# Moving the stream's buffers from 32 bytes below a 4 KB boundary of the partition onto one

## The chip, the cores and the metric

One core of one Trainium2 chip runs the kernel; the other cores are idle. The metric is the device time of the kernel in microseconds (us). Runs of the kernels before and after differ by about 0.05% among themselves, so a difference of 1% is far above the noise; of the experiments, e4 and e12 spread over 0.2% and e11 over 0.9%.

## The reference, cut to what matters

A decode step: layernorm and modulation, grouped-query attention over a long cache, then a small MLP. What costs is reading memory once: 134 MB of K and V cache and 44 MB of weights.

```python
x: (2, 1, 1024)
k_cache, v_cache: (2, 4, 32768, 128) bf16        # 67 MB each
w_mod (1024, 6144), wq (1024, 4096), wo (4096, 1024), w1 (1024, 3584), w2 (3584, 1024)
scores = einsum('bhqd,bhkd->bhqk', q, k) * Dh ** -0.5
p = softmax(scores); o = einsum('bhqk,bhkd->bhqd', p, v)
```

## The kernel before

All big loads form one stream, issued in a fixed order by SyncE (SP) into a ring of 160 KB a partition. Most loads are 2 MB: 128 partitions, 16 KB each in one contiguous run. A load waits only until the tiles that overlap its place in the ring have been read.

```python
RING = 160 * 1024
...
ident = sb("ident", [128, 128], BF16)          # the first of some 60 small tensors
# ... [cut] ...
KT_sb = [sb(f"KT_sb{i}", [128, 8, 128], BF16) for i in range(NKT)]

arena = nc.alloc_sbuf_tensor("arena", [128, RING], mybir.dt.uint8)   # comes last
abase = nc.lookup_mloc(arena).addr             # 61,408 = 15 * 4096 - 32
# ... [cut] ...
SLOT = {("K", 0): 0, ("K", 1): 1, ("V", 0): 2, ("V", 1): 3, ("K", 2): 4, ("V", 2): 5, ("K", 3): 6, ("V", 3): 7}

def add_kv(kind, i, cc):                       # 8192 keys, 64 to a partition: 16 KB in one run
    cache = A_k_cache if kind == "K" else A_v_cache
    b, g = i % 2, i // 2
    r0 = cc * CH_ROWS
    add((kind, i, cc), [TPC, D], cache[b, g][r0:r0 + CH_ROWS, :].rearrange("(p t) d -> p t d", p=128),
        SLOT[kind, cc] * 16 * KB, f"{kind}{cc}")
# ... [cut] ...
def need(*key):                                # issues the stream up to the item asked for
    ...
        T.dma("sp", lambda e, dst=dst, src=cur.src: e.dma_start(dst, src), key=cur.sem, writes=[cur.reg], frees=old)
```

The offsets of all items in the ring are multiples of 1 KB, and so are their rows (7 KB, 8 KB, 12 KB or 16 KB). So the place of `abase` modulo 1 KB is the place of every packet of the stream.

## Time and profile before

| | before |
|---|---|
| time, median of 3 runs | 430.73 us (430.69 to 430.78) |
| load queue q1, share of 16 engines' span | 98.4% |
| bytes moved, mean rate | 178.6 MB, 416 GB/s |
| PE / DVE / ACT busy | 68% / 38% / 36% |

From the page of the kernel before: DMA busy share and rate in 40 equal slices of the span, the packets, the load queue (q1), the chain of waits by engine, and the issues of the K loads (KB each, median us from issue to landing).

```profile
DMA  8999999999999999999999999999999999999993
GB/s 330 428 418 418 428 419 429 422 424 425 428 428 428 428 428 425 428 428 428 427 428 428 428 425 429 426 429 425 429 426 427 428 428 427 428 424 412 419 416 155
DMA packets 14471, 178.61 MB, mean 416 GB/s; under 512 B 1768, under 2 KB 1775, under 8 KB 2799
...
q1 hardware_dynamic: 14112, 178.27, 98.4%
...
DMA 79%; PE 17%; ACT 1%; SPq 1%; DVE 1%; issue 1%; DVEq 0%; ACTq 0%
...
K<-in_A_k_cache_dram SPq DMA_DIRECT2D x32, 2048.0 KB, 32.2
```

Every slice but the first and the last has the DMA engines busy. A 2 MB load takes about 4.9 us of them but lands 32 us after its issue, so several loads always queue. The table of stages (busy us and instruction count of PE, PEld, DVE, ACT, POOL, then granted clock, DMA share, GB/s) says the same for the steady stretch of the kernel before: all engines have slack, DMA has none.

```profile
120.00:350.00 230.00, 178.81 (x3441) 155.04 (x3434) 112.69 (x214) 108.63 (x191) 1.14 (x6) 0.90 1.01 427
```

### The profile page before, as it was taken

How to read it: one execution, taken by the hardware profiler on the slowest of the kernel's cores; microseconds unless marked ns; L12 is line 12 of the kernel's file. 1: busy time of each engine (PE TensorE's matmuls, PEld its weight loads, DVE VectorE, ACT ScalarE, POOL GpSimd, SP SyncE). 2: the span in 40 equal slices, each digit the busy share in tenths (PEclk: the TensorE clock that was granted, in tenths of full speed). 3: DMA queues.
4: the chain of work that ended last, by engine and by line, in shares of the span. 5: the costliest groups of instructions: out<-in, count | busy, mean ns of one | idle time of the engine just before them, and what ended most of it. 6: DMA issues, size and time to landing. Idle time of an engine off the chain costs nothing.

```text
span 429.0 us, 13364 instructions
## 1 busy us (share of the span) xinstructions
PE 289.7 (68%) x6035; PEld 253.2 (59%) x6035; DVE 162.9 (38%) x340; ACT 155.0 (36%) x266; POOL 2.8 (1%) x17
## 2 busy tenths in 40 slices
PE   0643368968997689678777858895878671644644
PEld 0632368956875688477576837784866661243543
DVE  0200026534574366247436524761564343102100
ACT  1100016438556338244634543481437335100100
POOL 1000000000000000000000000000000000000000
PEclk9999999868999979889969898897989886655555
DMA  8999999999999999999999999999999999999993
GB/s 330 428 418 418 428 419 429 422 424 425 428 428 428 428 428 425 428 428 428 427 428 428 428 425 429 426 429 425 429 426 427 428 428 427 428 424 412 419 416 155
DMA packets 14471, 178.61 MB, mean 416 GB/s; under 512 B 1768, under 2 KB 1775, under 8 KB 2799
## 3 DMA queue, kind: packets, MB, share of 16 engines
q1 hardware_dynamic: 14112, 178.27, 98.4%
q8 instruction: 16, 0.26, 0.2%
q10 hardware_dynamic: 334, 0.02, 0.1%
q14 instruction: 9, 0.07, 0.0%
HBM read 178.28 MB, written 0.00 MB: 416 GB/s over the span
## 4 chain that ended last, share of the span: by engine, by line
DMA 79%; PE 17%; ACT 1%; SPq 1%; DVE 1%; issue 1%; DVEq 0%; ACTq 0%
DMA K<-in_A_k_cache_dram 59%; PE psKT L476 11%; DMA wo<-in_A_wo_dram 8%; DMA w<-in_B_w_dram 7%; DMA wmod<-in_w_mod_dram 5%; PE psS L488 3%; PE psO L518 1%; SPq L373 1%; ACT KT_sb L480 1%; PE psS L612 0%; ACT E_sb L509 0%; PE psO L646 0%; ACT L509 0%; DVE KT_sb L482 0%; PE psM L422 0%
## 5 line engine op out<-in xcount | busy, mean ns | idle before, releaser
L476 PE MATMUL psKT<-ident,K 128*128 128x128 bf16 x2048 | 175.2, 238 | 42.5 <-DMA K<-in_A_k_cache_dram 42.5
L476 PEld LDWEIGHTS psKT<-ident,K 128*128 128x128 bf16 x2048 | 134.3, 106 | 52.8 <-DMA K<-in_A_k_cache_dram 49.3
L480 ACT ACTIVATE KT_sb<-psKT 128x1024 bf16<-128x1024 bf16 x96 | 97.9, 1020 | 175.3 <-PE psKT L476 175.1
L482 DVE COPY KT_sb<-psKT 128x1024 bf16<-128x1024 bf16 x160 | 108.5, 690 | 121.7 <-PE psKT L476 120.6
L488 PE MATMUL psS<-qcur,KT_sb 128*128 128x8 bf16 x2048 | 88.8, 168 | 9.8 <-ACT KT_sb L480 7.1
L488 PEld LDWEIGHTS psS<-qcur,KT_sb 128*128 128x128 bf16 x2048 | 80.1, 99 | 15.5 <-ACT KT_sb L480 9.4
L518 PE MATMUL psO<-V,E_sb 128*32 128x512 bf16 x512 | 36.5, 412 | 3.8 <-DMA V<-in_A_v_cache_dram 3.0
L509 ACT ACTIVATE E_sb<-S_sb,negm 128x256 bf16<-128x256 f32 x64 | 32.3, 504 | 9.8 <-DVE negm L505 8.9
L493 DVE TENSOR_REDUCE m1c<-S_sb 128x8 f32<-128x512 f32 x32 | 21.9, 686 | 14.7 <-ACT S_sb L492 13.6
L492 ACT ACTIVATE S_sb<-psS 128x512 f32<-128x512 f32 x32 | 19.0, 592 | 13.3 <-PE psS L488 13.3
L518 PEld LDWEIGHTS psO<-V,E_sb 128*32 128x32 bf16 x512 | 11.6, 101 | 15.1 <-DMA V<-in_A_v_cache_dram 4.1
L447 PE MATMUL psS<-siluT,wmod 128*128 128x2 bf16 x384 | 11.2, 165 | 8.5 <-DMA wmod<-in_w_mod_dram 7.0
L455 PE MATMUL psO<-hT,wq 128*128 128x2 bf16 x256 | 7.5, 165 | 12.9 <-DMA wq<-in_A_wq_dram 12.9
L447 PEld LDWEIGHTS psS<-siluT,wmod 128*128 128x128 bf16 x384 | 10.9, 104 | 8.9 <-DMA wmod<-in_w_mod_dram 7.3
L612 PE MATMUL psS<-atT,wo 128*128 128x2 bf16 x256 | 7.5, 165 | 12.4 <-DMA wo<-in_A_wo_dram 12.4
L612 PEld LDWEIGHTS psS<-atT,wo 128*128 128x128 bf16 x256 | 7.1, 104 | 13.3 <-DMA wo<-in_A_wo_dram 13.3
L455 PEld LDWEIGHTS psO<-hT,wq 128*128 128x128 bf16 x256 | 7.1, 104 | 13.2 <-DMA wq<-in_A_wq_dram 13.2
L424 ACT ACTIVATE stat<-stat 128x2 f32<-128x2 f32 x3 | 0.6, 203 | 37.1 <-DVE stat L423 37.1
L646 PE MATMUL psO<-gT,w 128*128 128x2 bf16 x224 | 6.6, 165 | 9.8 <-DMA w<-in_B_w_dram 9.8
L646 PEld LDWEIGHTS psO<-gT,w 128*128 128x128 bf16 x224 | 6.3, 104 | 10.1 <-DMA w<-in_B_w_dram 10.1
L509 ACT ACTIVATION_READ_ACCUMULATOR E_sb<-S_sb,negm 128x1 f32 x64 | 12.1, 189 | 0.0
L628 PE MATMUL psS<-h2T,w 128*128 128x2 bf16 x224 | 7.8, 172 | 3.4 <-DMA w<-in_B_w_dram 2.2
(85 smaller groups left out, 86.1 us busy)
## 6 DMA issues: line engine op xcount, KB each, us to landing
K<-in_A_k_cache_dram SPq DMA_DIRECT2D x32, 2048.0 KB, 32.2
V<-in_A_v_cache_dram SPq DMA_DIRECT2D x32, 2048.0 KB, 35.7
wmod<-in_w_mod_dram SPq DMA_DIRECT2D x8, 1536.0 KB, 17.5
wq<-in_A_wq_dram SPq DMA_DIRECT2D x4, 2048.0 KB, 38.2
wo<-in_A_wo_dram SPq DMA_DIRECT2D x4, 2048.0 KB, 27.6
w<-in_B_w_dram SPq DMA_DIRECT2D x4, 1792.0 KB, 38.3
w<-in_B_w_dram SPq DMA_DIRECT2D x3, 2048.0 KB, 31.5
w<-in_B_w_dram SPq DMA_DIRECT2D x1, 1024.0 KB, 29.8
```

Source lines behind the costliest of these rows:

```text
L447: pe(lambda e, w=it.view, j=j, k=k: e.matmul(psS[0][:, 2 * j:2 * j + 2], lhsT=w[:, j * 128:(j + 1) * 128], rhs=siluT[:, :, k], start=(k == ...
L455: pe(lambda e, w=it.view, h=h, k=k: e.matmul(psO[:, 2 * h:2 * h + 2], lhsT=w[:, k % 2, h * 128:(h + 1) * 128], rhs=hT[:, k, :], start=(k = ...
L476: pe(lambda e, kq=kq, jj=jj, w=it.view, t=t: e.transpose(psKT[kq][:, jj * 128:(jj + 1) * 128], w[:, t, :], ident[:, :]), reads=[it.reg, "i ...
L480: act(lambda e, src=src: e.activation(KT_sb[g8][:, :, :], src, ACT.Copy), reads=[f"psKT{kq}"], writes=[f"KT_sb{g8}"], sem=f"ev{cc}_{g8}")
L482: dve(lambda e, src=src: e.tensor_copy(KT_sb[g8][:, :, :], src), reads=[f"psKT{kq}"], writes=[f"KT_sb{g8}"], sem=f"ev{cc}_{g8}")
L488: pe(lambda e, t=t, jj=jj: e.matmul(ps[:, t * HPG:(t + 1) * HPG], lhsT=KT_sb[g8][:, jj, :], rhs=qcur[:, :], start=True, stop=True), reads= ...
L492: act(lambda e: e.activation(Sc, ps[:, :].rearrange("p (t h) -> p h t", h=HPG), ACT.Copy), reads=[preg], writes=[f"S_sb{i % 2}_{cc}"], sem ...
L493: dve(lambda e: e.tensor_reduce(m1c[:, :, cc], Sc, AX.X, ALU.max), reads=[f"S_sb{i % 2}_{cc}"], writes=[f"m1c{cc}"])
L509: act(lambda e: e.activation(E_sb[:, :, h, :], S_sb[j][:, h, :].rearrange("p (u t) -> p u t", t=4), ACT.Exp, bias=negm[:, h:h + 1], scale= ...
L518: pe(lambda e, t4=t4, tg=tg, q=q: e.matmul(psO[32 * q:32 * q + 32, :], lhsT=E_sb[:, tg // 4, :, :].rearrange("p h t -> p (h t)"), rhs=it.v ...
L612: pe(lambda e, w=it.view, g=g, j=j, k=k: e.matmul(psS[0][:, 2 * k:2 * k + 2], lhsT=w[:, j, k * 128:(k + 1) * 128], rhs=atT[g][:, j, :], st ...
L646: pe(lambda e, w=it.view, q=q, j=j, k=k: e.matmul(psO[:, 2 * k:2 * k + 2], lhsT=w[:, q % 2, j * DM + k * 128:j * DM + (k + 1) * 128], rhs= ...
```

## The change

Its intent is that every write of the stream starts at a round address. Nothing is computed or loaded differently; the ring is allocated first, behind a pad that brings it to 20,480 = 5 * 4096, and the other tensors follow it.

```diff
     def sb(name, shape, dtype=FP32):
         return nc.alloc_sbuf_tensor(name, list(shape), dtype)
+
+    nc.alloc_sbuf_tensor("pad", [128, 3968], mybir.dt.uint8)
+    arena = nc.alloc_sbuf_tensor("arena", [128, RING], mybir.dt.uint8)
+    abase = nc.lookup_mloc(arena).addr
 
     ident = sb("ident", [128, 128], BF16)
...
     KT_sb = [sb(f"KT_sb{i}", [128, 8, 128], BF16) for i in range(NKT)]
 
-    arena = nc.alloc_sbuf_tensor("arena", [128, RING], mybir.dt.uint8)
-    abase = nc.lookup_mloc(arena).addr
-
```

## The prediction

> **What bounds the kernel.** The stream of DMA loads. The page gives load queue q1 98.4% of 16 engines' span, 178.27 MB, 416 GB/s on average. The table of stages by 10 us shows a DMA share of 0.99 to 1.03 in every stretch from 10 to 420 us, while PE is busy 68% of the span, DVE 38%, ACT 36%. The chain of waits is 79% DMA; its 17% PE are hops through a buffer that PE freed, not idle DMA engines: a 2 MB load takes about 4.9 us of the 16 engines but lands a median of 32 to 38 us after its issue, so six or seven loads are queued. Only some 3 us before the first load and 5 to 6 us after the last are not stream.
>
> **What the change does.** No instruction comes or goes. Every stream buffer moves from 32 bytes below a 4 KB boundary onto one; the other tensors shift by 128 bytes modulo 4 KB. So only the duration of a DMA packet can change.
>
> **Cost of a packet now**, from the trace's DMA packet records (medians): 7,168 B 275 ns, 8,192 B 313 ns, 12,288 B 464 ns, 16,384 B 614 ns. The slope is 27.2 B/ns an engine, 435 GB/s for 16: the fabric ceiling in the Trainium skill, "DMA: Bandwidth & Descriptors", section "Where 436 GB/s comes from"; the trace agrees to 0.1%. So one 32 B beat is 1.176 ns, and each packet has about 11.7 ns on top (10 beats), whatever its size. 16,384 B cross four 4 KB boundaries and 8,192 B two, at equal overhead: a crossing costs nothing measurable. Alignment can save only a part of those 10 beats.
>
> How much? The small loads of the start: 256 B to a 256 B-aligned place and 256 B to one 32 bytes beyond both take 18 ns, and 1,024 B to an unaligned place 46 ns; that is 7 beats over the data, with no effect of 256 B alignment. The large packets have 3 more. The same page, section "How a descriptor splits into AXI transactions", says that a transaction starts at a 256 B boundary, so a descriptor starting 32 B short of one spends a whole transaction on its first 32 B: up to 7 beats lost. The equal 18 ns speak against that for small writes, not for large ones.
>
> An engine handles about 792 stream packets (544 of 16 KB, 64 of 12 KB, 120 of 8 KB, 64 of 7 KB). Estimates from these numbers:
> - no effect: 430.7 us;
> - 3 beats saved: 792 x 3.5 ns = 2.8 us, 427.9 us;
> - 7 beats: 6.5 us, 424.2 us;
> - all 10: 9.3 us, 421.4 us, out of reach I believe.
>
> All of it lies on the critical path, since the queue never runs dry.
>
> **Prediction:** 428.0 us, 80% range 424.0 to 431.2. Faster by over 2%: 0.06; within 2%: 0.93; slower by over 2%: 0.01.
>
> **What would show it.** 16,384 B packets at about 610 ns instead of 614, the 7,168 and 8,192 B packets shorter by the same nanoseconds; steady slices at about 430 GB/s instead of 428; DMA share still about 1.0; mean durations on PE, DVE and ACT unchanged.
>
> **What would make it wrong.** An alignment that matters per transaction and not per packet (then the slope changes); packets split differently at an aligned address; a stream so fast that PE's buffer releases become the limit, seen as a DMA share under 1; engine reads of the arena that change with the address.

## More of the kernel before

The costliest groups of instructions of the kernel before (partitions x elements, count, then busy us, mean ns, idle before):

```profile
L476 PE MATMUL psKT<-ident,K 128*128 128x128 bf16 x2048 | 175.2, 238 | 42.5 <-DMA K<-in_A_k_cache_dram 42.5
L480 ACT ACTIVATE KT_sb<-psKT 128x1024 bf16<-128x1024 bf16 x96 | 97.9, 1020 | 175.3 <-PE psKT L476 175.1
L482 DVE COPY KT_sb<-psKT 128x1024 bf16<-128x1024 bf16 x160 | 108.5, 690 | 121.7 <-PE psKT L476 120.6
L518 PE MATMUL psO<-V,E_sb 128*32 128x512 bf16 x512 | 36.5, 412 | 3.8 <-DMA V<-in_A_v_cache_dram 3.0
```

PE, the busiest of the engines, waits 42.5 us for K loads at its costliest line.

## The result, and the profile after

| | before | after |
|---|---|---|
| time, median of 4 runs | 430.71 us (430.66 to 430.78) | 426.16 us (426.04 to 426.25) |
| ratio | | 0.9894, 95% interval 0.9877 to 0.9911 |
| q1, share of 16 engines' span | 98.4% | 98.6% |
| mean rate | 416 GB/s | 421 GB/s |

A ratio is the mean time of one kernel's runs over that of the other kernel's runs of the same rounds, so it is not quite the ratio of the medians quoted. The change is 1.1% faster, 4.55 us: well outside the noise.

From the page of the kernel after, the same lines:

```profile
DMA  8999999999999999999999999999999999999994
GB/s 329 429 425 422 435 426 426 431 424 433 428 434 429 434 431 430 431 431 432 432 432 429 433 426 435 428 432 432 429 434 428 432 432 430 431 428 420 426 427 176
DMA packets 14470, 178.61 MB, mean 421 GB/s; under 512 B 1767, under 2 KB 1774, under 8 KB 2798
...
q1 hardware_dynamic: 14112, 178.27, 98.6%
...
DMA 79%; PE 17%; ACT 1%; SPq 1%; DVE 1%; issue 1%; DVEq 0%; ACTq 0%
...
K<-in_A_k_cache_dram SPq DMA_DIRECT2D x32, 2048.0 KB, 31.8
```

The stages of the kernel after:

```profile
120.00:350.00 230.00, 181.74 (x3480) 157.82 (x3480) 114.00 (x214) 110.44 (x192) 1.04 (x6) 0.89 1.01 431
```

And its groups of instructions:

```profile
L477 PE MATMUL psKT<-ident,K 128*128 128x128 bf16 x2048 | 175.5, 238 | 39.7 <-DMA K<-in_A_k_cache_dram 39.7
L481 ACT ACTIVATE KT_sb<-psKT 128x1024 bf16<-128x1024 bf16 x96 | 97.8, 1019 | 169.5 <-PE psKT L477 169.3
L483 DVE COPY KT_sb<-psKT 128x1024 bf16<-128x1024 bf16 x160 | 108.3, 689 | 117.4 <-PE psKT L477 116.2
L519 PE MATMUL psO<-V,E_sb 128*32 128x512 bf16 x512 | 34.4, 394 | 4.1 <-DMA V<-in_A_v_cache_dram 3.3
```

The number and bytes of the stream's packets are the same, the queue is as full as before (share 1.01), and the same engines do the same work at the same speed; only the rate of the stream rose, from 427 to 431 GB/s. PE's wait for K shrank from 42.5 to 39.7 us: it was given its data a little sooner. The one group that moved, L518 from 412 to 394 ns, isn't the change's doing: in the run e2 below, aligned like this one, it is 419 ns.

What changed is in the records of single DMA packets. Their durations for the 8,704 stream packets of 16,384 B:

```
before:  612 ns x539   613 x815   614 x4873   619 x542   621 x1894   ...   mean 616.5
after:   611 ns x8675  (all but 29)                                         mean 611.8
medians before / after:  7,168 B 275 / 272    8,192 B 313 / 309    12,288 B 464 / 460
```

Before, 16 KB packets had two lengths, around 614 and around 621 ns; after, one.

**The length of a record is not what a packet costs.** A packet's record begins 3 to 4 ns before the one ahead of it on its engine ends. The records carry no engine number, but with that gap they can be chained: from 120 to 340 us this gives 16 chains, with eight data packets between two completion packets almost throughout. (A completion packet is the 4 B record that ends a load on an engine.) The chaining is inferred, and 88% of the packets before and 95% after have only one candidate for the next one, a record that begins 2 to 5 ns before their own ends. A count that needs no chaining agrees: 16 engines times 220 us, less 5.9 ns for each completion packet, over the 5,738 (before) and 5,786 (after) packets of 16 KB that start in this stretch, is 612.7 and 607.6 ns a packet. From start to start a packet then takes, in ns:

| packet | its bytes at 435.2 GB/s | before (mean) | after (median; the mean is within 0.6) |
|---|---|---|---|
| 7,168 B | 263.5 | 274.3 | 268 |
| 8,192 B | 301.2 | 311.4 | 306 |
| 12,288 B | 451.8 | 461.6 | 456 |
| 16,384 B | 602.4 | 612.8 | 607 |

The second column is the size divided by 27.2 B/ns. That is the slope of the last column (8,192 B more take 301 ns), and over 16 engines it makes 435.2 GB/s. After the change every size costs its bytes plus 4.2 to 4.8 ns. Before, it costs 5 to 6 ns more by the means, whatever the size. An engine has 544 + 64 + 120 + 64 = 792 stream packets (16, 12, 8 and 7 KB); with the means of both kernels (after: 607.55, 456.5, 306.4, 268.3) the sum is 544 x 5.2 + 64 x 5.1 + 120 x 5.0 + 64 x 6.0 = 4.1 us of the 4.55 measured. The rest, 0.4 us, stays unattributed.

### The profile page after: what moved, and what is told of

It is laid out like the page before. It is cut to its first block, busy times and chain, and to the rows that moved or that the text cites. A ratio compares the mean times of both kernels' runs of the same rounds, so it can differ in the third digit from the quotient of the medians.

```text
span 424.5 us, 13364 instructions
## 1 busy us (share of the span) xinstructions
PE 287.6 (68%) x6035; PEld 252.8 (60%) x6035; DVE 162.8 (38%) x340; ACT 155.1 (37%) x266; POOL 2.8 (1%) x17
## 3 DMA queue, kind: packets, MB, share of 16 engines
q1 hardware_dynamic: 14112, 178.27, 98.6%
## 4 chain that ended last, share of the span: by engine, by line
DMA 79%; PE 17%; ACT 1%; SPq 1%; DVE 1%; issue 1%; DVEq 0%; ACTq 0%
DMA K<-in_A_k_cache_dram 59%; PE psKT L477 11%; DMA wo<-in_A_wo_dram 8%; DMA w<-in_B_w_dram 7%; DMA wmod<-in_w_mod_dram 5%; PE psS L489 3%; PE psO L519 1%; SPq L374 1%; ACT KT_sb L481 1%; ACT E_sb L510 0%; PE psS L613 0%; PE psO L647 0%; ACT L510 0%; DVE KT_sb L483 0%; PE psM L423 0%
## 5 line engine op out<-in xcount | busy, mean ns | idle before, releaser
L477 PE MATMUL psKT<-ident,K 128*128 128x128 bf16 x2048 | 175.5, 238 | 39.7 <-DMA K<-in_A_k_cache_dram 39.7
L519 PE MATMUL psO<-V,E_sb 128*32 128x512 bf16 x512 | 34.4, 394 | 4.1 <-DMA V<-in_A_v_cache_dram 3.3
```

Source lines behind the costliest of these rows:

```text
L477: pe(lambda e, kq=kq, jj=jj, w=it.view, t=t: e.transpose(psKT[kq][:, jj * 128:(jj + 1) * 128], w[:, t, :], ident[:, :]), reads=[it.reg, "i ...
L519: pe(lambda e, t4=t4, tg=tg, q=q: e.matmul(psO[32 * q:32 * q + 32, :], lhsT=E_sb[:, tg // 4, :, :].rearrange("p h t -> p (h t)"), rhs=it.v ...
```

## The experiments

The theory: a write that starts off some boundary costs a fixed amount per packet. Open were which boundary, whether the new places of the other tensors matter, and whether the read side has a part.

**e1: the new order, the old alignment.**

```diff
-    nc.alloc_sbuf_tensor("pad", [128, 3968], mybir.dt.uint8)
+    nc.alloc_sbuf_tensor("pad", [128, 3936], mybir.dt.uint8)
```

> The new order of tensors, but the pad 32 bytes shorter, so the stream's buffers start 32 bytes below a 4 KB boundary again. If the start address is the cause (my theory): the time of before, 430.7 us, and 16,384 B packets spread again over 614 and 621 ns. If the order or the places of the other tensors are the cause (rival): about 426.2 us and 611 ns.

Measured: 430.62 us, ratio to before 1.0005 (0.9988 to 1.0021). The packets spread as before the change: 614 ns 4,880 times, 621 ns 1,893 times.

**e2: the old order, 32 bytes of pad in front of the ring.**

```diff
+    nc.alloc_sbuf_tensor("pad", [128, 32], mybir.dt.uint8)
     arena = nc.alloc_sbuf_tensor("arena", [128, RING], mybir.dt.uint8)
```

> The kernel before with 32 bytes put in front of the stream's buffers and nothing else moved: their start is 61,440, a multiple of 4 KB. Start address theory: 426.2 us, all 16,384 B packets 611 ns. Rival (order or places of the other tensors): 430.7 us.

Measured: 426.11 us, ratio 0.9898 (0.9881 to 0.9914); 8,676 of 8,704 packets at 611 ns. With e1 this settles it: the start address of the ring is the whole effect, and 32 bytes buy it.

**e3: 64 bytes above the boundary** (pad of 4,032).

> The change with the buffers 64 bytes above the 4 KB boundary: still 64-byte aligned, but not 128- or 256-byte aligned. If 64-byte alignment is all that counts: 426.2 us and 611 ns. If 256-byte transactions count: 16 KB then takes 65 of them and the packets lose about as much as before: 428 to 431 us. If the tiny first piece before a boundary costs (32 bytes only), then here the first piece to the next 256 B boundary is 192 bytes and the loss is small.

Measured: 429.82 us, ratio 0.9985 (0.9968 to 1.0001); packets at 613 (4,520) and 620 ns (1,826), 1 ns shorter than before. Alignment to 64 bytes buys 0.7 of the 4.5 us against the runs of before in the same rounds. A long first piece doesn't help either: the loss was expected to be small if a tiny first piece were the cost.

**e4: 32 bytes above the boundary** (pad of 4,000).

> The change with the buffers 32 bytes above the 4 KB boundary: the same 32-byte misalignment, but the piece before the next 256 B or 4 KB boundary is long and the piece of 32 bytes is at the end of the packet. If any start off 64 bytes costs: 430 to 431 us and 614 or more ns. If only the short first piece below a boundary costs: 426.2 to 427 us.

Measured: 430.78 us, ratio 1.0012 (0.9995 to 1.0029); packets at 614 (4,878) and 621 ns (1,897). The same loss above the boundary as below it. Being just short of a 4 KB boundary is not the cause.

**e5: 128 bytes above the boundary** (pad of 4,096).

> The change with the buffers 128 bytes above the 4 KB boundary. If the write is cut into 256 B pieces and a start inside one costs (now my theory, after 64 bytes turned out not to be enough): above 426.2 us, 428 to 430, and 16,384 B packets over 611 ns. If 128-byte alignment is enough: 426.2 us and 611 ns.

Measured: 429.87 us, ratio 0.998 (0.9963 to 0.9996); the packets spread over 611 to 622 ns, mean 615.5. 128-byte alignment buys 0.8 us and isn't enough.

**e6: 256 bytes below the boundary** (pad of 3,712).

> The change with the buffers 256 bytes below the 4 KB boundary. If 256-byte pieces are what counts: 426.2 us and 611 ns, although every packet now starts just below a 4 KB boundary as it did before the change. If the 4 KB boundary counts (the change's own wording): 429 to 431 us.

Measured: 426.06 us, ratio 0.9893 (0.9877 to 0.991); 8,673 packets at 611 ns. Its stages:

```profile
120.00:350.00 230.00, 185.24 (x3483) 161.36 (x3484) 113.92 (x214) 110.12 (x192) 0.95 (x5) 0.87 1.01 431
```

The same 431 GB/s as after the change, although nearly all packets again cross their first 4 KB boundary after 256 bytes. What the change bought is 256-byte alignment; the 4 KB boundary has no part in it.

**e7 and e8: the same bytes in twice as many packets, aligned and not.** Each K and V load reads two runs of 8 KB a partition. Keys are permuted alike in K and V, so the result stays right. Both traces have 18,304 packets of 8,192 B and 512 of 16,384 B, as intended. e7 is this edit on the kernel after, e8 on the kernel before.

```diff
-            cache[b, g][r0:r0 + CH_ROWS, :].rearrange("(p t) d -> p t d", p=128)
+            cache[b, g][r0:r0 + CH_ROWS, :].rearrange("(u p t) d -> p u t d", u=2, p=128)
...
+            if cur.key[0] in "KV":
+                dst = dst.rearrange("p (u t) d -> p u t d", u=2)
```

> The change with each K and V load reading two 8 KB runs a partition in place of one of 16 KB (keys permuted alike in K and V, so the result is right): 512 more packets an engine at aligned addresses. From the 309 ns of an aligned 8 KB packet against 611 of 16 KB: 7 ns times 512 = 3.6 us more, 429.8 us.

> The same split of the K and V loads in the kernel before, 32 bytes below the boundary. If the loss is one fixed amount per packet (my theory): two packets of 315.9 ns for one of 616.5, 15.2 ns times 512 = 7.8 us more, 438.5 us, so the gap to the aligned split is about 8.7 us instead of 4.5. If the loss goes with bytes or with crossings inside the packet (rival): the gap stays about 4.5 us, so 434 us.

Measured: e7 428.47 us, ratio 0.9948 (0.9931 to 0.9965); e8 435.75 us, ratio 1.0119 (1.0102 to 1.0136). The stages of e7, then of e8:

```profile
120.00:350.00 230.00, 180.10 (x3465) 156.67 (x3462) 113.69 (x215) 109.46 (x191) 1.15 (x6) 0.90 1.01 428
```

```profile
120.00:350.00 230.00, 179.84 (x3368) 155.66 (x3360) 110.75 (x210) 106.93 (x188) 1.15 (x6) 0.87 1.01 421
```

The gap between unaligned and aligned is 7.3 us instead of 4.55: 1.60 times as large, with 1.65 times as many packets (1,304 against 792). The rival said that it would stay. So the loss goes with packets, not with bytes or with what they cross inside.

Both expectations were too high, by 1.3 and 2.8 us, and by this the lengths of records were found out. 512 more packets an engine cost 2.3 us aligned, 4.5 ns each, where the records (309 x 2 against 611) said 7; unaligned they cost 5.0 us, 9.9 ns each, where the records said 15. The start-to-start times give it: 2 x 306 - 607 = 5 ns, and 2 x 311.4 - 612.8 = 10.0 ns. The 3 to 4 ns by which records overlap had been counted as a cost.

**e9 and e10: the read side.** K and V are read from 224 bytes further on in HBM, so the numbers are wrong (the last chunk is read from 32 bytes earlier, the same place modulo 256; the comparison with the reference can't tell these keys and values from the right ones). e9 has the aligned ring of the kernel after, e10 the ring of the kernel before, whose writes also start 224 bytes past a 256-byte place.

```diff
-        add((kind, i, cc), [TPC, D], cache[b, g][r0:r0 + CH_ROWS, :].rearrange("(p t) d -> p t d", p=128),
+        e0 = ((b * G + g) * S + r0) * D
+        e0 += 112 if (b, g, cc) != (B - 1, G - 1, NCH - 1) else -16
+        flat = cache.rearrange("b g s d -> (b g s d)")
+        add((kind, i, cc), [TPC, D], flat[e0:e0 + CH_ROWS * D].rearrange("(p t d) -> p t d", p=128, d=D),
```

> The change, with the K and V loads reading from 224 bytes past a 256-byte place of HBM (32 bytes below the next; wrong result on purpose, same bytes in all), destinations aligned. If only the place of the write costs: 426.2 us and 611 ns. If the read side pays as well, or if read and write must lie alike modulo 256 bytes: 512 K and V packets an engine at about 5.3 ns (what the misalignment cost per packet in the steady stretch), 2.7 us more, 428.9 us.

> The kernel before (writes 32 bytes below a 256-byte place) with the same shift of the K and V reads, so that read and write lie alike modulo 256 bytes for K and V (wrong result on purpose). If only the place of the write costs: 430.7 us. If what costs is a read and a write that lie differently: K and V at 611 ns, the weights as before, 427.6 to 428 us. If each side pays on its own: about 433.4 us.

Measured: e9 426.07 us, ratio 0.9894 (0.9877 to 0.991), 8,669 packets at 611 ns; e10 430.82 us, ratio 1.0003 (0.9987 to 1.002), packets at 614 (4,883) and 621 ns (1,895). Moving the reads changes nothing, and letting reads and writes lie alike doesn't help: only where the write starts counts. One reservation: the trace doesn't show where the caches lie in HBM. If they didn't start at a 256-byte place, both runs would have unaligned reads.

**e11: fewer packets.** If a packet costs 4.5 ns beyond its bytes, longer packets must gain a little more. K and V are loaded 4 MB at a time on top of the change, 32 KB a partition in one run, into four slots of 32 KB instead of eight of 16 KB.

```diff
-    SLOT = {("K", 0): 0, ("K", 1): 1, ("V", 0): 2, ("V", 1): 3, ("K", 2): 4, ("V", 2): 5, ("K", 3): 6, ("V", 3): 7}
+    SLOT = {("K", 0): 0, ("V", 0): 2, ("K", 1): 4, ("V", 1): 6}
-        r0 = cc * CH_ROWS
-        add((kind, i, cc), [TPC, D], cache[b, g][r0:r0 + CH_ROWS, :]
+        r0 = cc * 2 * CH_ROWS
+        add((kind, i, cc), [2 * TPC, D], cache[b, g][r0:r0 + 2 * CH_ROWS, :]
+    def half(kind, i, cc):
+        whole, it = need(kind, i, cc // 2), Item()
+        it.reg, it.view = whole.reg, whole.view[:, cc % 2 * TPC:(cc % 2 + 1) * TPC, :]
+        return it
... (w1 at 64, 80, 32, 48 KB of the ring and w2 at 96, 112, 128, 144 KB)
```

> A candidate to beat both: the change with K and V in loads of 4 MB, 32 KB a partition in one run, four slots in place of eight; the last weights sit elsewhere in the ring. 256 packets an engine fewer at 4.6 ns (what an extra aligned packet cost in the aligned split) and 32 completion packets of 9 ns fewer: 1.5 us less, 424.7 us, if the coarser slots don't starve the queue (DMA share would drop under 1). If the packet cost is the 8.6 ns of the packet records: 2.5 us less, 423.7 us.

Measured: 431.41 us (429.14 to 433.04), ratio 1.0 (0.9969 to 1.0032): a miss, and unsteady. The packets are as hoped, 1,209 ns from start to start for 32 KB, 4.3 ns over the bytes. But the queue ran dry twice, as its stages show:

```profile
90.00:100.00 10.00, 9.04 (x179) 8.51 (x178) 5.83 (x13) 5.20 (x6) 0.19 (x1) 0.85 0.76 289
120.00:340.00 220.00, 171.66 (x3296) 146.43 (x3293) 108.72 (x208) 104.83 (x187) 1.14 (x6) 0.88 1.00 432
350.00:360.00 10.00, 10.00 (x178) 8.05 (x171) 4.37 (x7) 3.67 (x4) 0.00 (x0) 0.70 0.54 233
```

Half of the last stretch is idle DMA. With four slots, a load at the head of the queue waits longer for its slot, and everything behind it waits too: one K load at 76 to 93 us, the last V load until 360 us. SyncE's issues show it (start, duration with the waits inside, loads issued):

```profile
75.58 17.31 SPq L374 DMA_DIRECT2D K<-in_A_k_cache_dram  x2
319.54 40.44 SPq L374 DMA_DIRECT2D V<-in_A_v_cache_dram  x3
```

Why the time varies so much from run to run was not looked into.

**e12: the same, with the dry spells taken away by order.** Loads whose places are free go ahead of the two that have to wait. The edit is shown against e11; the loop that added the wo loads is replaced by single calls (cut).

```diff
-    early = [("V", 0), ("K", 0), ("K", 1), ("V", 1)]
+    early = [("V", 0), ("K", 0), ("V", 1), ("K", 1)]
...
             if kind == "V":
+                if (i, cc) == (NBG, 1):
+                    add_wo(0, 128)
+                    add_wo(1, 144)
                 add_kv("V", i - 1, cc)
```

> The 32 KB kernel again, with its two dry spells of the queue (DMA share 0.76 at 90 to 100 us and 0.54 at 350 to 360 us) taken away by order alone: the second V load of the first pair goes ahead of a K load that has to wait, and two weight loads, whose places in the ring are free, go ahead of the last V load. If the dry spells were why the last kernel didn't gain: 424.6 us (426.1 less 256 packets at 4.6 ns and 32 completions at 9 ns), DMA share 0.98 or more in every stretch. If it is the longer packets themselves that are slower: 427 us or more with a full DMA share.

Measured: 424.84 us (424.72 to 425.65), ratio to before 0.9868 (0.9851 to 0.9884); the result is right. Its stages:

```profile
90.00:100.00 10.00, 7.26 (x120) 6.51 (x118) 4.80 (x10) 3.92 (x5) 0.19 (x1) 0.83 1.00 427
120.00:340.00 220.00, 176.10 (x3395) 152.10 (x3393) 110.86 (x212) 107.37 (x190) 1.13 (x6) 0.88 1.00 433
350.00:360.00 10.00, 7.19 (x137) 5.66 (x135) 6.69 (x15) 3.57 (x5) 0.00 (x0) 0.84 0.97 415
```

Both dry spells are gone (the last stretch has 0.97, a hair under the 0.98 expected, and so have 80 to 90 and 270 to 280 us), and the time is within 0.3 us of the 424.6 worked out from 4.6 ns a packet. It beats the kernel before and, by 1.3 us of the medians, the kernel after. These two weren't run side by side, but all four runs of each lie apart (424.72 to 425.65 against 426.04 to 426.25). e12 differs from the kernel after in the order of loads too, but the packets alone can account for it by the medians: 2 x 607 - 1,209 = 5 ns for each of 256 pairs an engine is 1.3 us.

## Why the prediction was right or wrong

- *DMA bounds the kernel, and all that a packet loses is lost on the critical path.* Right. Share 1.01 before and after in the steady stretch, and 4.1 of the 4.55 us are the sum over packets.
- *Only the duration of a packet can change.* Right. e1 and e2 show that the places of the other tensors don't matter, and the groups on PE, ACT and DVE keep their durations.
- *The loss is per packet, and crossing 4 KB costs nothing.* Right. e6 and the pair of e7 and e8 show it directly.
- *The size: 3 beats, 3.5 ns a packet, 428.0 us.* The direction and mechanism held, but the gain was 4.55 us where 2.7 was forecast. That 426.16 us lies in the range says little, since 424.0 to 431.2 also held the case of no effect. (A beat is 32 B, 1.176 ns at 27.2 B/ns.) The term that was mis-sized is "3 beats saved: 792 x 3.5 ns = 2.8 us". It was taken from medians, 614 ns against a floor of 7 beats over the data. That the small loads' floor holds for 16 KB packets was assumed, and it came out right: 512 beats and 7 make 610.6 ns, and the records say 611. But 22% of the packets were not at 614 but at 621 ns, and a sum needs the mean. The mean of the start-to-start times gives 5.2 ns for 16 KB packets. The second group stood in the records of before and was passed over.
- *"Each packet has about 11.7 ns on top (10 beats)".* Too much: records of neighbouring packets overlap by 3 to 4 ns. The cost beyond the bytes was about 10 ns before and is 4.2 to 4.8 ns now. The overlap is in both kernels, so it hardly touches the difference; it did spoil the expectations of e7 and e8.
- *"The equal 18 ns speak against that for small writes, not for large ones".* The caution was right. Small loads to two different places modulo 256 bytes took equally long, and yet large ones do pay for it. Why the small ones don't stays open; so does why some packets lose 3 ns and others 10.
- The estimate of 7 lost beats, from the rule for transactions at 256-byte boundaries, overstates the loss: 5.2 ns are 4.4 beats of 1.176 ns. That rule speaks of bytes that are fetched (see the list at the end), that is of reads; the prediction carried it over to writes. And starts at 32, 64 or 224 bytes past a 256-byte place lose nearly the same (means 616.5, 615.6 and 616.5 ns), where wasted beats would grow with the distance.

## What to carry to other kernels

Where a kernel is bound by DMA loads, see that each packet's write starts at a multiple of 256 bytes in the partition: 32 bytes of padding bought 1.1% here, and a start 256 bytes below a 4 KB boundary served as well as one on it. Cost a packet by the time from its start to the next one's start, and take means: a record's length and a median both misled here. Longer packets gain a little more (1.3 us in e12), but bigger buffers release later, so look for stretches in which the queue runs dry and put loads with free places ahead of the ones that wait.

## What the Trainium skill lacked or had wrong

- "SBUF — State Buffer", section "Operand start alignment", is about what is allowed, as it says itself, and no page that was read gives a speed for where a DMA's write starts. Here a start off 256 bytes costs 5 to 6 ns a packet from 7 to 16 KB: 612.8 against 607.6 ns for 16 KB, 430.7 against 426.2 us for the kernel.
- "DMA: Bandwidth & Descriptors", section "How a descriptor splits into AXI transactions", says that a descriptor starting off 256 bytes fetches bytes it doesn't use. The 256-byte grain shows here for the write. For the read, moving the source by 224 bytes changed nothing (e9, 426.07 us), with the reservation about the caches' own address; and the loss doesn't grow with the bytes below the start.
- The same page, section "Why small descriptors are slow (HBM only)", gives a fixed cost of about 3 cycles per packet. The aligned packets show 4.2 to 4.8 ns over their bytes, 3.6 to 4.1 cycles of 1.176 ns, also at 16 and 32 KB.
- The same page, section "Where 436 GB/s comes from", says that for loads from HBM the HBM side, about 358 GB/s, binds. This one core alone held 431 GB/s, near the fabric ceiling of 435 that the page states, and its packets are explained by that ceiling to within 5 ns. The same section also reports 425 GB/s for a 16 MB load, so the sentence about 358 needs a condition that it doesn't state; the other cores were idle here.
- None of the pages read says that the profile's records of neighbouring DMA packets on an engine overlap; here by 3 to 4 ns, which makes a 16 KB packet look 611 ns long where the next starts after 607.
